# Paced operand work in a fused attention and two-layer gated network: rates by kind of pass, earlier stores, charged borders, and another order in the prologue

## The chip, the cores and the metric

One core of one Trainium2 chip runs the whole program. The metric is the device time in microseconds (us) of one execution; lower is better. A run gives one time, and the median of the runs is compared. A profiled execution has a time of its own and a span, which runs from the first to the last instruction that the profiler saw.

## The reference

Chunked attention over 4 batches, 8 heads, 768 positions and head size 64, then two networks over the 3072 tokens of width 512.

```python
for c in range(24):                       # chunks of 32 queries
    k_full = concat([mem_k, k[l_start:r_end]])   # 8 memory keys, 16 left, 32, 8 right
    a = softmax(scale * q_c @ k_full.T)
    out[c] = a @ v_full
x = out.transpose(0, 2, 1, 3).reshape(3072, 512)
x = (sigmoid(x @ w_gate) * (x @ w_val)) @ w_out        # d_ff 1536
h = x @ w_in                                           # d_ff 2048
y = (h * sigmoid(h)) @ w_out2
```

q, k and v are float32; the weights are float64, arrive as pairs of 32-bit words, and the kernel turns each into a float32.

## The kernel before

**Operands.** A product is made of three TensorE passes: each operand is split into a high part (rounded to the fp32r type by a cast on ScalarE) and a low part (the difference, on VectorE), and high x high, high x low and low x high are added in PSUM. `Unit.rebias` (a Prelu on ScalarE, L124) and `Unit.join` (a shift, L134, and a shift with or, L137, on VectorE) make a float32 of it; `high` and `rest` split it.

**Stages.** The first network takes the tokens in blocks of 512. Four of its six blocks go the plain way (the loop at L1260): for each of 12 column tiles f a gate projection (`proj`, PSUM tile pg), a value projection (pv), the sigmoid, the product `gated`, and the out projection of the tile before (`emit_out1`, PSUM tile y). The attention of the coming block is worked off beside it at fixed steps (`run_events`: "meet" is scores, maximum and difference, then "exp", "norm", and "turn", a transpose on TensorE). The last two blocks of the first network, and all of the second, go in `pair2` (products into c, L1060) and `out2` (products into o, L1224): seven products of sums of quarter matrices instead of eight, in the manner of Strassen. Passes are numbered by b (-1 for the first network's rest, 0 to 2 for the second network) and by p; for b = -1 each p has a pass of kind "g" and one of kind "v".

**Operand work.** The sums of weights that these products need (S1 to S4) are made on the way, in small portions between the other work, and stored to DRAM: in blocks 1 to 3 for the first network's weights (`PairC`) and w_in (`Pair2` "i"), in the passes b = -1 and b = 0 for w_out2 (`Pair2` "o", tiles stg_w2o, fo, coo, DRAM tensor w2o_d). A planner, `Pace`, hands out the portions while the program is written out, so it sets nothing but the order of instructions on each engine. A generator `steps` of an item yields the cost in us of its next VectorE portion, or None to end the step. `Pace.go(us)` is called once in each third of a tile, and at three beats of each pass. It first issues the stores that are LAG steps old, adds us to a credit (`due`, at most 3.2), and lets the item go on while the credit pays. The casts need a free one of four (in stage one five) tiles co: a tile is free again REST = 3 steps after its store was issued.

A "Pair2" item is charged 1.15 us for each of two joins, 0.8 for each of two halves of the sums, 0.7 for three low parts and 0.4 for the last. `early` issues the next item's Prelus, before its first join.

`Pace.finish` hands out what is left at once. For w_out2 it stands ahead of pass b = 0, p = 6 (L1337), since the memory of the prep pool is needed there:

```python
if b == 0 and p == NPAIR - 2:
    prep.finish()
    pp_cm.__exit__(None, None, None)
```

**A pass.** `pair2` emits, in order: product c1 with A11 and its copy s1 (ScalarE, L1095); c3 with S1 and its copy s5 (L1099), to which GpSimd adds s1 (L1100); c2 with S2 and the sum u2 (VectorE, L1025); beat 0; c1 goes on with A12; c2 with S3 and the sum into s5; beat 1; c3 with S4; c2 with A22; beat 2. A product is 6 matmuls. c1 goes on in the same PSUM tile that s1 is copied from, and c2 in that which u2 is read from. The weights of a pass come from DRAM through a ring of five buffers (wr, `next_granule`); loads, stores and ring loads all go through SyncE's queue (SP) in the order of the program. `tail_of` gives the next pass the work that forms an operand of `out2`; where there is none it gives a function that does nothing:

```python
return lambda: None
```

In `pair2` the result of that call is `rest`, and beat 0 hands out 0.0 where `rest` holds.

**Prologue.** The first four attention tiles and the first weights are done in an order written out by hand (PROLOGUE); after it x is split in `x_high` (ScalarE, L561) and `x_low` (VectorE, L564) and the first tile's two projections run together in `proj_both` (L346). units[1] is the value weight of tile 0. `Pace` is made at block 1; its first act is `ones[0].ahead()`, which on GpSimd adds up the high and low part of two gate weights (L670).

**Borders.** At f = 11 of a block `split_x` splits the next block's x (four casts on ScalarE, L96, and four differences on VectorE, L99); at f = 0 of the next block four y tiles are copied (L908, L910) and stored (L911).

Of the kernel before, what the change touches and what calls it, by code (L numbers as in the profile page):

```python
# [22 lines left out]
KT = DM // P  # L23
# [9 lines left out]
NPAIR = NF2 // 2  # L33
# [18 lines left out]
DVE_US = {"meet": 2.1, "norm": 1.75}  # L52
PREP1, PREP_END, PREP1X = 1.9, 130, 1.2
PREP2 = {"g": (0.7, 2.2, 1.5), "v": (0.8, 1.1, 0.3), "l": (0.8, 2.3, 1.7)}
# [3 lines left out]
def moe_kernel(ctx: ExitStack, tc: tile.TileContext, qh, kh, vh, wg, wv, wo, w2i, w2o, out):  # L58
# [282 lines left out]
    def proj_both(os, ws, x, n):  # L341

        steps = [(i, kt, p) for i in range(2) for kt in range(KT) for p in ((0, 0), (1, 0))]
        steps += [(i, kt, (0, 1)) for i in range(2) for kt in range(KT)]
        for i, kt, (pw, px) in steps:
            nc.tensor.matmul(  # L346
                os[i][:, :n],
                ws[i][:, pw, kt * P : (kt + 1) * P],
                x[kt][:, px, :n],
                start=kt == 0 and (pw, px) == (0, 0),  # L350
                stop=kt == KT - 1 and px == 1,
            )
# [34 lines left out]
    with tc.manual_schedule():  # L387
# [182 lines left out]
        x_low(0)  # L570
        units[1].high()
        x_high(2)
        units[1].rest()
        x_high(3)
        x_low(1)
# [69 lines left out]
        class PairC:  # L645
# [33 lines left out]
            def ahead(self):  # L679
                even, odd = (w_t[2 * self.p + j][:, "gv".index(self.k)] for j in range(2))  # L680
                self.store(A11, even)
                self.store(A22, odd[:, :, 256:])
                self.t = [
                    p1.tile([P, 512], F32, tag=f"u{j}", name=f"tc{self.k}{self.p}_{j}")
                    for j in range(2)
                ]
                self.whole(self.t[0], even, nc.gpsimd)
                self.whole(self.t[1], odd, nc.gpsimd)
# [30 lines left out]
        class Pair2:  # L719
# [31 lines left out]
            def steps(self, pace):  # L751
                k, p = self.k, self.p
                if not self.ready:
                    self.rebias()
                    yield None
# [39 lines left out]
        class Pace:  # L795

            LAG, REST = 2, 3

            def __init__(self, items, tags):
# [8 lines left out]
                if ones:  # L808
                    ones[0].ahead()

            def early(self):
                coming = self.urgent or self.items
                if coming and isinstance(coming[0], Pair2):
                    coming[0].rebias()
# [35 lines left out]
            def go(self, us):  # L850
                self.step += 1
                while self.fifo and self.fifo[0][0] <= self.step - self.LAG:
                    self.put()
                self.due = min(self.due + us, 3.2)
                while self.next is not False and self.next <= self.due:
# [186 lines left out]
        def pair2(b, p, fill, tail, kind=""):  # L1042
# [43 lines left out]
            def beat(n):  # L1086
                if b < 0 or b == 0 and p < NPAIR - 2:
                    us = PREP2[kind if kind else "l"][n]
                    prep.go(0.0 if rest and n == 0 or b < 0 and p == 0 and kind == "g" else us)
# [6 lines left out]
            if tail and early:  # L1096
                tail()()
# [29 lines left out]
            def tail_of():  # L1127
# [6 lines left out]
                return lambda: None  # L1134
# [125 lines left out]
        for bi, n in enumerate(BLOCKS1[:NB1]):  # L1260
            last = bi == NB1 - 1
            if bi == 1:
                prep = Pace(items, ["stg2", "stg3", "co0", "co1", "co2"])
            for f in range(NF1):
                it = 3 * (bi * NF1 + f)

                def steps(i):
# [3 lines left out]
                    else:  # L1271
                        prep.go((PREP1 if it + i < PREP_END else PREP1X) - sum(DVE_US.get(w, 0) for w, t in events.get(it + i, [])))
# [12 lines left out]
                else:  # L1285
                    proj(psg, U1["g", f].u, x, n, late=(0, 1) if f == 0 else (1, 0) if bi else None)
# [38 lines left out]
        prep = Pace([Pair2("o", p, pool) for p in range(NPAIR)], ["co0", "co1", "co2", "co3"])  # L1325
        xgen = iter(())
        for b in range(-1, NB2):
# [14 lines left out]
            tail()()  # L1342
# [3 lines left out]
            def beside(m):  # L1346
                nonlocal xgen
                if b + 1 == NB2:
                    return
                if m == 0:  # L1350
# [81 lines left out]
```

## Time and profile before

| | us |
|---|---|
| median of 3 runs | 1113.5 |
| lowest and highest run | 1112.88, 1116.63 |
| the profiled execution, time | 1114.81 |
| the profiled execution, span | 1113.0 |
| TensorE busy | 1087.2 |
| VectorE busy | 759.7 |
| ScalarE busy | 533.6 |
| GpSimd busy | 97.0 |

The profiled execution lies 1.31 us above the median of the runs, and 1.81 us of it lie outside the span. Engines are named PE (TensorE; PEld is its weight load), DVE (VectorE), ACT (ScalarE), POOL (GpSimd) and SP (SyncE); a q behind the name is the engine's issuing of a DMA or its wait ahead of an instruction. A wait in brackets names the idle time of the engine ahead of the row and what ended it.

### The profile page before, as it was taken

What the parts mean: (1) busy time and instruction counts of PE and PEld (TensorE: products, weight loads), DVE (VectorE), ACT (ScalarE), POOL (GpSimd) and SP (SyncE); (2) the same over time, 40 slices, a digit from 0 to 9 for tenths busy, and PEclk for the clock granted to TensorE, in tenths of its full rate; (3) what the DMA queues carried; (4) which work ended last, traced back from release to release, by engine and by line L of the source; (5) the groups of instructions that cost most, each with busy time, mean ns of one, the idle gap of its engine ahead of it and who ended that gap; (6) DMA issues with size and microseconds to landing.
All of it is one profiled execution on the core that took longest, in us unless ns stands there. A gap on an engine that the chain in (4) does not pass through costs nothing.

```text
span 1113.0 us, 18985 instructions
## 1 busy us (share of the span) xinstructions
PE 1087.2 (98%) x7580; PEld 890.2 (80%) x7580; DVE 759.7 (68%) x1132; ACT 533.6 (48%) x791; POOL 97.0 (9%) x74
## 2 busy tenths in 40 slices
PE   7999999999999999999999999699999999999998
PEld 4888888878888788888888888588888888888887
DVE  8988776777766766657769866468833489443665
ACT  6767555454445453443444556354443454344442
POOL 0000001002111001011111011000011110011000
PEclk9999999999999999999999999899999999999999
DMA  8788788697986897678998699765765766655551
GB/s 319 259 276 302 263 298 296 224 323 271 320 294 222 308 303 275 223 266 311 301 315 313 206 336 336 278 268 190 244 200 194 274 217 218 208 199 208 203 218 71
DMA packets 106248, 288.03 MB, mean 259 GB/s; under 512 B 8624, under 2 KB 39344, under 8 KB 95408
## 3 DMA queue, kind: packets, MB, share of 16 engines
q1 hardware_dynamic: 105872, 286.43, 73.5%
q8 instruction: 60, 0.98, 0.4%
q10 hardware_dynamic: 288, 0.39, 0.1%
q14 instruction: 28, 0.23, 0.1%
HBM read 210.24 MB, written 76.55 MB: 258 GB/s over the span
## 4 chain that ended last, share of the span: by engine, by line
PE 93%; DVE 3%; ACT 2%; DMA 1%; issue 0%; SPq 0%; DVEq 0%; ACTq 0%
PE o L1224 21%; PE c L1060 20%; PE pg L359 11%; PE pv L359 11%; PE y L104 4%; PE y L106 4%; PE y L108 4%; PE sx L308 1%; PE sx L220 1%; PE o_-1_0_6435 L1224 1%; PE o_-1_1_6436 L1224 1%; PE c_-1_4g L1060 1%; PE c_-1_2v L1060 1%; PE c_-1_5v L1060 1%; PE c_-1_5g L1060 1%; PE c_-1_3v L1060 1%
## 5 line engine op out<-in xcount | busy, mean ns | idle before, releaser
L1060 PE MATMUL c<-xp,wr 128*128 128x512 f32 x1008 | 231.3, 392 | 10.3 <-ACT s L1095 10.3
L1060 PEld LDWEIGHTS c<-xp,wr 128*128 128x128 f32 x1008 | 190.7, 189 | 50.3 <-ACT s L1095 10.7
L1224 PE MATMUL o<-gf,wr 128*128 128x512 f32 x1008 | 229.0, 389 | 0.0
L1224 PEld LDWEIGHTS o<-gf,wr 128*128 128x128 f32 x1008 | 189.3, 188 | 39.2
L359 PE MATMUL pv<-x,w 128*128 128x512 f32 x564 | 139.0, 396 | 1.1 <-DVE sg L374 1.1
L359 PE MATMUL pg<-x,w 128*128 128x512 f32 x564 | 136.2, 391 | 0.9 <-ACT sg L369 0.9
L1167 DVE TENSOR_TENSOR gf<-g,gf 128x1024 fp32r<-128x1024 f32 x84 | 104.0, 1241 | 46.6 <-ACT gf L1163 46.1
L1163 ACT CAST gf<-g 128x1024 fp32r<-128x1024 f32 x84 | 88.1, 1052 | 87.1 <-PE o L1224 69.8
L359 PEld LDWEIGHTS pg<-x,w 128*128 128x128 f32 x564 | 105.5, 188 | 23.4 <-ACT sg L369 1.4
L359 PEld LDWEIGHTS pv<-x,w 128*128 128x128 f32 x564 | 104.1, 188 | 24.8 <-DVE sg L374 2.1
L1025 DVE TENSOR_TENSOR s<-c,s 128x512 f32<-128x512 f32 x48 | 33.1, 690 | 53.0 <-PE c L1060 52.6
L1100 POOL TENSOR_TENSOR s<-s,s 128x512 f32<-128x512 f32 x24 | 34.3, 1430 | 333.2 <-ACT s L1099 333.2
L1028 DVE TENSOR_TENSOR g<-g,g 128x1024 f32<-128x1024 f32 x48 | 59.6, 1241 | 0.0
L369 ACT ACTIVATE sg<-pg 128x512 f32<-128x512 f32 x48 | 28.6, 596 | 59.9 <-PE pg L359 46.8
L379 DVE TENSOR_TENSOR g<-sg,g 128x512 fp32r<-128x512 f32 x48 | 33.9, 706 | 34.3 <-ACT g L376 34.3
L376 ACT CAST g<-sg 128x512 fp32r<-128x512 f32 x48 | 29.8, 620 | 55.1 <-DVE sg L374 55.1
L1031 ACT ACTIVATE g<-s 128x512 f32<-128x512 f32 x48 | 30.3, 632 | 47.1 <-DVE s L1025 47.1
L1025 DVE TENSOR_TENSOR u<-c,s 128x512 f32<-128x512 f32 x24 | 16.6, 690 | 50.1 <-PE c L1060 46.6
L269 ACT ACT_TABLE_LOAD x21 | 26.9, 1283 | 36.6 <-DVE e L261 34.8
L104 PE MATMUL y<-g,wor 128*128 128x512 f32 x144 | 40.1, 400 | 0.0
L106 PE MATMUL y<-g,wor 128*128 128x512 f32 x144 | 38.7, 390 | 0.0
L108 PE MATMUL y<-g,wor 128*128 128x512 f32 x144 | 38.6, 390 | 0.0
(602 smaller groups left out, 1579.1 us busy)
## 6 DMA issues: line engine op xcount, KB each, us to landing
wr<-w2o_d SPq DMA_DIRECT2D x42, 1024.0 KB, 4.8
wr<-w2i_d SPq DMA_DIRECT2D x24, 1024.0 KB, 5.3
wor<-wo_d SPq DMA_DIRECT2D x36, 512.0 KB, 6.2
wr<-w2i_d SPq DMA_DIRECT2D x24, 768.0 KB, 4.5
w2o_d<-coo SPq DMA_DIRECT2D x56, 256.0 KB, 7.0
w2i_d<-coi SPq DMA_DIRECT2D x24, 512.0 KB, 6.2
wr<-wc_d SPq DMA_DIRECT2D x12, 1024.0 KB, 6.5
v<-in_vh_dram SPq DMA_DIRECT2D x21, 512.0 KB, 5.4
```

Of the source, the lines that this page charges most:

```text
L104: nc.tensor.matmul(o, w_hi, x_hi, start=first, stop=False)
L106: nc.tensor.matmul(o, w_hi, x_lo, start=False, stop=False)
L108: nc.tensor.matmul(o, w_lo, x_hi, start=False, stop=last)
L359: nc.tensor.matmul(o[:, :n], w[:, pw, kt * P : (kt + 1) * P], x[kt][:, px, :n], start=i == 0, stop=i == len(steps) - 1,)
L379: nc.vector.tensor_tensor(out=g[:, 1, :n], in0=sg[:, :n], in1=g[:, 0, :n].bitcast(F32), op=ALU.subtract)
L1025: nc.vector.tensor_tensor(out=o, in0=a, in1=b_, op=ALU.add)
L1028: nc.vector.tensor_tensor(out=o, in0=a, in1=b_, op=ALU.subtract)
L1060: nc.tensor.matmul(o, w[:, pw, m, kt * P : (kt + 1) * P], X[i][:, px, kt], start=first and j == 0, stop=j == 5, skip_group_check=not first,)
L1100: nc.gpsimd.tensor_tensor(out=s5, in0=s5, in1=s1, op=ALU.add)
L1163: nc.scalar.copy(f[:, 0], src)
L1167: nc.vector.tensor_tensor(out=f[:, 1], in0=src, in1=f[:, 0].bitcast(F32), op=ALU.subtract)
L1224: nc.tensor.matmul(c[at[i], dp], w[:, pw, pl, dp * P : (dp + 1) * P], f[:, px, pl], start=i in (A11, S1, S2) and pp == 0 and j == 0, stop= ...
```

## The change

It edits the planner, its rates, the prologue and two orders of matmuls.

- Rates: stage one's step goes from 1.9 to 2.15 us; a step with `split_x` is charged 2.4 more, the second step of tile 0 of a block 1.4 more. The passes of b = -1 and b = 0 get rates "g", "v" and "rest"; b = 0 takes "rest" for p = 0 and for a pass that really has a `rest`, else "g". `tail_of` returns None where there is nothing to do.
- `Pace` for w_out2 gets lag 1 instead of 2 and a credit of at most 2.8 instead of 3.2; a call with 0.0 now only issues stores, and `out2` of b = -1 makes three such calls. Prelus aren't issued at beat 2.
- Prologue: `x_high(2)` and `x_high(3)` go ahead of the value weight's cast, `x_low(1)` ahead of its low part. The first `ahead` goes from GpSimd to VectorE.
- `proj_both` takes the value weight's high parts for all four kt ahead of its low ones; in block 0 the gate projection takes the weight's low part last.

```diff
-DVE_US = {"meet": 2.1, "norm": 1.75}
-PREP1, PREP_END, PREP1X = 1.9, 130, 1.2
-PREP2 = {"g": (0.7, 2.2, 1.5), "v": (0.8, 1.1, 0.3), "l": (0.8, 2.3, 1.7)}
+DVE_US = {"meet": 2.1, "norm": 1.75, "split": 2.4, "y": 1.4}
+PREP1, PREP_END, PREP1X = 2.15, 130, 1.2
+PREP2 = {"g": (0.9, 2.6, 1.8), "v": (1.0, 1.3, 0.7), "rest": (0.0, 0.9, 1.3)}
...
     def proj_both(os, ws, x, n):
-        steps = [(i, kt, p) for i in range(2) for kt in range(KT) for p in ((0, 0), (1, 0))]
+        steps = [(0, kt, p) for kt in range(KT) for p in ((0, 0), (1, 0))]
+        steps += [(1, kt, p) for p in ((0, 0), (1, 0)) for kt in range(KT)]
         steps += [(i, kt, (0, 1)) for i in range(2) for kt in range(KT)]
...
         x_low(0)
+        x_high(2)
+        x_high(3)
         units[1].high()
-        x_high(2)
+        x_low(1)
         units[1].rest()
-        x_high(3)
-        x_low(1)
         units[2].rebias()
...
-                self.whole(self.t[0], even, nc.gpsimd)
-                self.whole(self.t[1], odd, nc.gpsimd)
+                self.whole(self.t[0], even, eng)
+                self.whole(self.t[1], odd, eng)
...
                 if not self.ready:
+                    while not pace.act:
+                        yield None
                     self.rebias()
...
-            LAG, REST = 2, 3
-            def __init__(self, items, tags):
+            REST = 3
+            def __init__(self, items, tags, lag, cap):
+                self.lag, self.cap, self.act = lag, cap, True
...
                 if ones:
-                    ones[0].ahead()
+                    ones[0].ahead(nc.vector)
...
-                if coming and isinstance(coming[0], Pair2):
+                if self.act and coming and isinstance(coming[0], Pair2):
                     coming[0].rebias()
...
-            def go(self, us):
+            def go(self, us, act=True):
                 self.step += 1
-                while self.fifo and self.fifo[0][0] <= self.step - self.LAG:
+                self.act = act
+                while self.fifo and self.fifo[0][0] <= self.step - self.lag:
                     self.put()
-                self.due = min(self.due + us, 3.2)
-                while self.next is not False and self.next <= self.due:
+                self.due = min(self.due + us, self.cap)
+                while us and self.next is not False and self.next <= self.due:
...
-                    us = PREP2[kind if kind else "l"][n]
-                    prep.go(0.0 if rest and n == 0 or b < 0 and p == 0 and kind == "g" else us)
+                    us = PREP2["rest" if rest or b == 0 and p == 0 else kind or "g"][n]
+                    prep.go(0.0 if b < 0 and p == 0 and kind == "g" else us, n < 2)
...
-                return lambda: None
+                return None
...
-                prep = Pace(items, ["stg2", "stg3", "co0", "co1", "co2"])
+                prep = Pace(items, ["stg2", "stg3", "co0", "co1", "co2"], 2, 3.2)
...
+                        if (f, i) == (NF1 - 1, 2) and not last:
+                            names.append("split")
+                        if (f, i) == (0, 1):
+                            names.append("y")
+                        us = PREP1 if it + i < PREP_END else PREP1X
+                        prep.go(us - sum(DVE_US.get(w, 0) for w in names))
...
-                    proj(psg, U1["g", f].u, x, n, late=(0, 1) if f == 0 else (1, 0) if bi else None)
+                    proj(psg, U1["g", f].u, x, n, late=(0, 1) if f == 0 else (1, 0))
...
-        prep = Pace([Pair2("o", p, pool) for p in range(NPAIR)], ["co0", "co1", "co2", "co3"])
+        prep = Pace([Pair2("o", p, pool) for p in range(NPAIR)], ["co0", "co1", "co2", "co3"], 1, 2.8)
...
+                if b < 0 and m in (3, 8, 14):
+                    prep.go(0.0)
```

## Rows read from the trace of the kernel before

**Rows 1.** The page: busy time of each engine, its share of the span, instructions.

```profile
PE 1087.2 (98%) x7580; PEld 890.2 (80%) x7580; DVE 759.7 (68%) x1132; ACT 533.6 (48%) x791; POOL 97.0 (9%) x74
```

**Rows 2.** TensorE's waits: us in total, times, longest.

```profile
PE c L1060 <- ACT s L1095: 10.3, 1, 10.3
...
PE pt L292 <- DVE e L287: 0.7, 3, 0.3
...
PE c_-1_4v L1060 <- ACT s_-1_4v L1095: 0.4, 1, 0.4
```

**Rows 3.** Stretches: length, busy time (instructions) by engine, clock, DMA share, GB/s.

```profile
464.54:582.43 117.89, 117.44 (x518) 96.73 (x517) 76.40 (x126) 47.26 (x82) 15.52 (x12) 1.00 0.85 294
...
639.65:728.39 88.74, 78.45 (x338) 64.51 (x337) 52.77 (x87) 43.25 (x73) 10.35 (x8) 0.94 0.87 304
804.55:880.71 76.16, 76.16 (x338) 63.10 (x337) 28.96 (x38) 31.21 (x50) 11.99 (x8) 1.00 0.59 200
```

**Rows 4.** Timeline, 696 to 713 us: start, length, engine, line, operation, tiles.

```profile
697.23 15.18 SPq L746 DMA_DIRECT2D w2o_d<-coo  x14
...
706.81 0.62 ACT L777 CAST coo<-fo 128x512 fp32r<-128x512 f32 x1 [7.81 <-DMA w2o_d<-coo]
...
710.51 0.58 ACT L1095 COPY s<-c 128x512 f32<-128x512 f32 x1
...
711.14 2.08 PE L1060 MATMUL c<-xp,wr 128*128 128x512 f32 x4 [10.29 <-ACT s L1095]
```

**Rows 5.** Stretches in the prologue and after the long wait.

```profile
25.00:29.30 4.30, 2.96 (x7) 2.38 (x8) 4.11 (x8) 4.12 (x7) 0.00 (x0) 0.60 0.77 287
...
705.20:715.40 10.20, 4.26 (x10) 3.43 (x11) 5.23 (x6) 4.46 (x8) 1.28 (x1) 0.50 0.81 276
```

**Rows 6.** Timeline of the prologue's end.

```profile
23.22 1.25 PE L346 MATMUL pg<-x,w 128*128 128x512 f32 x4 [0.40 <-ACT x L561]
26.34 2.08 PE L346 MATMUL pg<-x,w 128*128 128x512 f32 x4 [1.87 <-ACT x L561]
...
32.37 0.84 PE L359 MATMUL pg<-x,w 128*128 128x512 f32 x3
...
23.46 1.66 DVE L137 SCALAR_TENSOR_TENSOR t_wv<-stg_wv 128x512 int32<-128x512 int32 x1
...
22.55 1.14 ACT L561 CAST x<-x 128x512 fp32r<-128x512 f32 x2 [0.61 <-DVE x L317]
...
23.18 1.39 POOL L670 TENSOR_TENSOR tcg<-w 128x512 f32<-128x512 f32 x1 [21.87 <-DVE w L147]
```

**Rows 7.** The tile stg_wv up to 60 us: ns least, median, most.

```profile
L137 DVE SCALAR_TENSOR_TENSOR t_wv<-stg_wv x5: 692/693/1656, 23.5 to 54.5; 128x512 int32<-128x512 int32 x5
```

**Rows 8.** Timeline at the border of blocks 0 and 1, VectorE.

```profile
137.82 0.43 DVE L134 TENSOR_SCALAR stg_w2i<-stg_w2i 128x512 int32<-128x512 int32 x1 [2.74 <-DMA stg_w2i<-in_w2i_dram]
```

**Rows 9.** Timeline at the border of blocks 2 and 3.

```profile
354.35 2.92 PE L359 MATMUL pg<-x,w 128*128 128x512 f32 x12
...
353.32 2.18 ACT L96 CAST x<-x 128x512 fp32r<-128x512 f32 x4
...
367.23 1.29 DVE L670 TENSOR_TENSOR tc<-wor 128x512 f32<-128x512 f32 x2
...
367.98 0.33 SPq L883 DMA_DIRECT2D wor<-wo_d  x1
...
374.58 3.03 PE L359 MATMUL pg<-x,w 128*128 128x512 f32 x12 [0.95 <-ACT sg L369]
378.67 3.03 PE L359 MATMUL pv<-x,w 128*128 128x512 f32 x12 [1.06 <-DVE sg L374]
```

**Rows 10.** The page: a group of sums (busy, mean ns), and the stores of coo.

```profile
L1025 DVE TENSOR_TENSOR s<-c,s 128x512 f32<-128x512 f32 x48 | 33.1, 690 | 53.0 <-PE c L1060 52.6
...
w2o_d<-coo SPq DMA_DIRECT2D x56, 256.0 KB, 7.0
```

**Rows 11.** The tile stg_w2o: its loads, from issue to landing.

```profile
DMA to landing us min/median/max: 3.7/6.7/7.6
```

More of the change, by code (lines that the diff above doesn't have):

```diff
@@ L677, in begin, with ahead @@
                 self.whole(self.t[1], odd, nc.vector)
-            def ahead(self):
+            def ahead(self, eng=None):
+                eng = eng or nc.gpsimd
                 even, odd = (w_t[2 * self.p + j][:, "gv".index(self.k)] for j in range(2))
@@ L1096, in pair2 @@
             if tail and early:
-                tail()()
+                (tail() or int)()
             prod(c3, S1, True)
@@ L1271, in steps @@
                     else:
-                        prep.go((PREP1 if it + i < PREP_END else PREP1X) - sum(DVE_US.get(w, 0) for w, t in events.get(it + i, [])))
+                        names = [w for w, t in events.get(it + i, [])]
+                        if (f, i) == (NF1 - 1, 2) and not last:
[4 more added lines that the diff above has]
+                        prep.go(us - sum(DVE_US.get(w, 0) for w in names))
                     if xgen is not None and (it + i) % 3 != 1:
@@ L1341, in moe_kernel @@
                     tail = pair2(b, p, None, tail)
-            tail()()
+            (tail() or int)()
             if b < 0:
```

## The prediction

> **What bounds the kernel now.** I read the page first: TensorE is busy for 1087.2 of 1113.0 us [rows 1], so what a change of order can win is at most its 26 us of idle time, and what it loses to a lower clock. Then TensorE's waits [rows 2]: one of 10.3 us holds over a third of that; of the small ones two matter below, 0.7 and 0.4. Then stretches cut at the borders of the stages [rows 3]: a stage of eight passes takes 76.16 us where nothing is in the way (804.55 to 880.71), and the stage of b = 0, with the same matmuls, 88.74 us. The difference of 12.58 us is the largest thing to win. The timeline there [rows 4] shows whose it is: ScalarE sat idle 7.81 us for a store of coo to land, then did the last casts (L777), then the copy s1 (L1095) that TensorE needed before it could go on at 711.14, after 10.29 us. SyncE issued 14 such stores in 15.18 us. This is `finish`: the last item of w_out2 was not done when pass p = 6 came, and its casts, which need tiles whose stores have only just been issued, stand in ScalarE's queue ahead of s1. The other 12.58 - 10.29 = 2.29 us are clock: from 705.2 to 715.4 it was 0.50, the level of 1.2 GHz, after 4.3 us without a matmul [rows 5].
>
> The prologue's end comes second [rows 6]: the 24 matmuls of `proj_both` run from 23.22 to the next projection at 32.37, though at the usual pace (76.16 us for 336, 0.227 each) they take 5.4. TensorE waited 1.87 us for a cast of x, and the clock was 0.60 on the mean over the next 4.3 us [rows 5].
>
> **The planner.** I step its credit through the beats by hand. An item of w_out2 costs 2 x 1.15 + 2 x 0.8 + 3 x 0.7 + 0.4 = 6.4, eight cost 51.2. Before, `lambda: None` is a true value, so beat 0 hands out nothing in any pass with a predecessor: b = -1 gives 5 x (2.2 + 1.5) + 6 x (1.1 + 0.3) = 26.9, b = 0 gives 4.8 + 5 x 4.0 = 24.8. That is 51.7 for 51.2, and steps lost to busy tiles use up more than the rest: the last item's casts are left for `finish`, as the rows show. After, b = -1 gives 3 x 5.3 (g at p = 1, 3, 5) + 2 x 2.2 (p = 2, 4, with a real rest) + 6 x 3.0 = 38.3, b = 0 gives 3 x 2.2 + 3 x 5.3 = 22.5: 60.8 in all. Stepped through with the four tiles, the last low part falls in beat 2 of p = 4 and the last store in beat 0 of p = 5; `finish` finds nothing. The stores and the loads of the moved items are cheap here, since they aren't new.
>
> **Part by part.**
>
> *The wait at finish:* -12.6 us, idle time and clock together. If a remnant stayed and the clock alone came back it would be 2.3; I see none, so 12.6.
>
> *Prologue:* while GpSimd adds up a gate weight (23.18, 1.39 us), VectorE's L137 on the value weight takes 1.66 us instead of 0.69 [rows 6, 7], and on ScalarE the cast of that weight, and behind it those of x(2) and x(3), wait for it. With `ahead` on VectorE and x(2), x(3) first, ScalarE's casts run on from 22.55 at about 0.55 each [rows 6] and end at 24.75; the value weight is joined at 23.46 + 0.69 = 24.15, cast by 25.4, its low part done by 26.05. TensorE takes the gate's eight matmuls until 25.25, the value's eight until 27.2, then the eight with low x, the last of which are done at 27.35: an end near 29.0 instead of 32.4. The next projection needs its weight's high part: join after `x_low(3)`, 28.5, cast 29.1, so it starts near 29.1. That is -3.3 with the clock at its upper level throughout. If the clock falls as before (a mean of 0.60 over 4.3 us [rows 5] is 3.4 us at half, from about 25.9 on), 1.7 of this is lost: bounds -1.6 and -3.7 (all that 9.15 us exceed 5.44 by). The hole of 1.87 us ahead of the fall shrinks to 0.2, so I take -3.3. (The Trainium skill, TensorE: Matmul & The Clock Gate, Part 1, has the clock follow how busy the engine has lately been. By that rule the fall can also come from the thinly filled time before 23 us, which the change leaves, and the sum would be 1.7 smaller; no row tells the two apart.) The two additions moved to VectorE, some 0.65 each, fall at the start of block 1, where it waits 2.74 us for the first load of w_in [rows 8]; without that cover they cost 1.3.
>
> *Border of blocks 2 and 3:* the y stores stand behind a load of w_out (L883, 367.98) that waits for VectorE's L670 (367.23), and VectorE is late by the joins and sums handed out at that border; the sigmoid needs a y tile's buffer and TensorE waits 0.95 and 1.06 [rows 9]. With the charges these portions go elsewhere: two joins and four sums, some 3.8 us, leave the way between, so both waits go, -2.0. Against it, stepping stage one, the credit saved up at step 1 of that tile now pays a join, both sums and two casts ahead of `split_x`. The casts need the sums, and end 1.2 us later than now; x's first cast (353.32 now, [rows 9]) is then ready near 355.1, and the projection that starts at 354.35 waits 0.8, and 0.4 more at the transpose: +1.2, against two of the three waits at a transpose now (0.7 together, [rows 2]), some 0.5. Net -1.3; bounds -2.5 (no late casts) and +0.7 (late casts and the y stores still blocked). At the border of 1 and 2 a cast leaves the same chain: -0.3, the third of those waits.
>
> *Prelus not at beat 2:* the wait of 0.4 us at p = 4 [rows 2] is the copy s1 behind two Prelus: -0.4.
>
> *Matmul orders:* the same matmuls; nothing, beyond the prologue.
>
> *More work in b = -1:* per pass VectorE has four sums of 0.69 [rows 10], in "v" four products as long, and 5.3 or 3.0 of portions: 8.1 and 8.5 of the 9.52 us that 42 matmuls take. ScalarE is fuller, but not full (47.26 of 117.89 us now, [rows 3]). DMA: 2.1 MB of loads and about 2.0 MB of stores move into the stretch 464.5 to 582.4, which now moves 34.7 MB (294 GB/s, share 0.85, [rows 3]): 38.8 MB, 329 GB/s, share 0.95. It fits, narrowly. New waits of 0 to 5 us can follow (rival 1 has the place); I take 0.5.
>
> **Sum:** 12.6 + 3.3 + 1.3 + 0.3 + 0.4 - 0.5 = 17.4. The profiled execution would take 1114.81 - 17.4 = 1097.4; it lies 1.31 above the median of the runs shown, 1113.5, and against that the forecast is 1096.1 us.
>
> **Rivals.**
>
> 1. *The Prelu waits for its load (the side that is slower).* In the "g" passes of p = 1, 3, 5 the next item's load is handed out at beat 0 and its Prelus at beat 1 of the same pass; before, a whole pass lay between. By SyncE's order the load can go out 0.45 us into the pass; it lands in 6.7 us, at most 7.6 [rows 11], and ScalarE comes to the Prelus near 9.0. Behind them stand two sigmoids and the next pass's s1, which TensorE needs 13.6 us in (9.52 and 18 matmuls); so nothing is lost until a load takes 10 us. The fuller DMA speaks for it, the measured 7.6 against. At 13 us it costs 3 x 3 = 9, and 1105 comes out; from about 16 us on it takes back all 17.4, and each wait over 4.3 us brings the clock down as [rows 5] show (2.3 more each): at 17 us 3 x 9.3 = 27.9, some 1124. The same holds for casts that wait for stores: they now follow them by three beats, 9.5 us, against 7.0 [rows 10].
>
> 2. *The change doesn't do what it says:* an item is still open at p = 6, because a tile is busy where I counted it free. Then part of the wait stays; half of it gives 1096.1 + 6.3 = 1102.4.
>
> 3. *The clock falls in the prologue all the same:* against it that the hole ahead of the fall is nearly closed, for it that the matmuls before 23.22 [rows 6] stay as few as they were: 1096.1 + 1.7 = 1097.8.
>
> 4. *VectorE late through GpSimd.* Each pass has an addition on GpSimd of s1 to s5; portions moved into b = -1 can meet it and be held as L137 was, by 0.97 us [rows 7]. A portion of beat 2 held so ends about 4.5 us into the next pass, and u2, due at 5.4, takes 0.69: late by no more than 0.3 us. In eleven passes that is up to 3.3: 1099.4. (The Trainium skill, SBUF — State Buffer, "Who interferes with whom", says that a VectorE instruction with two SBUF inputs and a GpSimd one that reads SBUF exclude each other for a whole instruction. By that rule every sum and low part can be held, not L137 alone, which is why this rival has a chance of its own.)
>
> **How the numbers follow.** As forecast, with the small terms within their bounds (1093.7 to 1098): 0.62. Rival 3: 0.12. Rival 4: 0.07. Rival 2: 0.05. Rival 1 in part (1098 to 1108): 0.09; in full, slower: 0.04; near no change, from the same place: 0.01. The range of 8 in 10 takes in the first three and the mild part of rival 1: 1093.5 to 1101. A measurement of this kernel tells about 0.3%, 3.3 us, from no change: faster 0.95, same 0.01, slower 0.04.
>
> **What would show it.** In the profile after: the stage of b = 0 takes about 76.2 us from its first to its last c matmul, and no cast L777 waits for a store ahead of s1; the clock stays at 1.00 there. L137 on the first value weight takes 0.69 us, the first projection at L359 starts near 29. No wait of a projection on the sigmoid at the border of blocks 2 and 3, but one near 0.8 us on a cast of x. The stretch of b = -1 has a DMA share near 0.95. The forecast is wrong if waits on s1 show up in the passes after "g" of p = 1, 3 or 5, if `finish` still finds casts to do, or if the attention tiles' loads, which share SyncE's queue, come late in stage one.

## The result, and the profile after

The changed kernel takes 1100.06 us (median of 5 runs, 1099.36 to 1100.85) beside 1113.5 for the kernel before: a ratio of 0.9872, 95% interval 0.9853 to 0.989. That is 13.4 us less; the forecast was 17.4 less, and 1100.06 lies inside its range near the upper end. The profiled execution took 1100.55 us with a span of 1098.8. Line numbers have moved: L346 is now L347, L359 is L360, L561 is L562, L633 is L634, L641 is L642, L670 is L671, L777 is L781, L1025 is L1031, L1060 is L1066, L1095 is L1101, L1100 is L1106, L1167 is L1173, L1224 is L1230.

The page, busy time by engine, answers to [rows 1]:

```profile
PE 1085.0 (99%) x7580; PEld 888.0 (81%) x7580; DVE 758.0 (69%) x1134; ACT 534.1 (49%) x791; POOL 95.0 (9%) x72
```

TensorE's waits (us in total, times, longest) answer to [rows 2]:

```profile
PE c_-1_3g L1066 <- DVE u_-1_3g L1031: 0.9, 1, 0.9
PE c_-1_5g L1066 <- DVE u_-1_5g L1031: 0.9, 1, 0.9
...
PE pg L360 <- ACT x L96: 0.4, 1, 0.4
...
PE c L1066 <- ACT s L1101: 0.4, 2, 0.2
```

The wait of 10.3 us is gone, and five small waits for other engines that were not there before have come (the last row holds two); a sixth new one, 0.5 us in the attention's products px (L308), has no releaser in the profile. The stretches of [rows 3], cut at the same matmuls (columns as there), say where the time went:

```profile
460.35:579.75 119.40, 117.55 (x517) 96.69 (x517) 85.32 (x144) 49.42 (x87) 16.58 (x12) 1.00 0.91 315
636.98:714.14 77.16, 76.76 (x337) 62.91 (x337) 44.96 (x69) 39.04 (x65) 10.36 (x8) 1.00 0.87 297
790.30:866.46 76.16, 76.16 (x337) 63.06 (x337) 28.96 (x38) 31.24 (x50) 11.99 (x8) 1.00 0.59 199
```

Block 0's eight passes lost 11.58 us (88.74 to 77.16) and their clock is 1.00. The passes of b = -1 grew by 1.51 (117.89 to 119.40): VectorE has 18 instructions and 8.92 us more to do there. The start of that stretch moved from 464.54 to 460.35, 4.19 earlier, which is the prologue and stage one. So -4.19 + 1.51 - 11.58 = -14.26, and that is the whole difference of the two profiled executions, 1114.81 - 1100.55.

The prologue's end, the timeline of TensorE, VectorE and ScalarE, answers to [rows 6]:

```profile
24.67 2.30 PE L347 MATMUL pg<-x,w 128*128 128x512 f32 x8 [0.40 <-ACT x L562]
26.81 2.04 PE L347 MATMUL pv<-x,w 128*128 128x512 f32 x8
...
30.50 3.00 PE L360 MATMUL pg<-x,w 128*128 128x512 f32 x12
...
24.92 0.69 DVE L137 SCALAR_TENSOR_TENSOR t_wv<-stg_wv 128x512 int32<-128x512 int32 x1
...
24.00 2.19 ACT L562 CAST x<-x 128x512 fp32r<-128x512 f32 x4 [1.28 <-DVE x L317]
```

From the first matmul to the next projection it is 5.83 us in place of 9.15, without a hole; but the first matmul comes at 24.67, not at 23.22, and so the projection starts only 1.87 earlier. On the tile stg_wv L137 now takes 0.69 throughout, against the 1.66 of [rows 7]. The two additions that moved to VectorE cost nothing: at the start of block 1 it still waits 1.63 us for the load of w_in ([rows 8] have 2.74).

The border of blocks 2 and 3 (TensorE, ScalarE), against [rows 9]:

```profile
353.27 3.22 PE L360 MATMUL pg<-x,w 128*128 128x512 f32 x12 [0.41 <-ACT x L96]
...
372.75 2.88 PE L360 MATMUL pg<-x,w 128*128 128x512 f32 x12
375.47 2.89 PE L360 MATMUL pv<-x,w 128*128 128x512 f32 x12
...
351.56 1.14 ACT L781 CAST coi<-fi 128x512 fp32r<-128x512 f32 x2 [0.29 <-DVE fi L634]
352.60 2.18 ACT L96 CAST x<-x 128x512 fp32r<-128x512 f32 x4
```

The waits of 0.95 and 1.06 us are gone; the casts of coi stand ahead of x's casts, and the projection waits 0.41 us for them, as the forecast had it, at half its size.

Last, VectorE, GpSimd and TensorE where the new wait of 0.93 us arises (timeline, pass p = 3 "g"):

```profile
523.45 0.69 DVE L1090 TENSOR_TENSOR g-1_1_21_5887<-s_-1_2v,g-1_1_21_5887 128x512 f32<-128x512 f32 x1
524.05 1.84 DVE L634 TENSOR_TENSOR fo<-fo 128x256 f32<-128x256 f32 x2
525.82 0.68 DVE L1031 TENSOR_TENSOR u_-1_3g<-c_-1_3g,s_-1_3g 128x512 f32<-128x512 f32 x1
...
523.66 1.61 POOL L1106 TENSOR_TENSOR s_-1_3g<-s_-1_3g 128x512 f32<-128x512 f32 x1 [8.28 <-ACT s_-1_3g L1105]
...
526.55 1.66 PE L1066 MATMUL c_-1_3g<-xp-1_3_5399,wr 128*128 128x512 f32 x6 [0.93 <-DVE u_-1_3g L1031]
```

Two sums of w_out2 (L634), handed out at beat 2 of the v pass, stand ahead of u2. The first started 0.39 us after GpSimd began to add s1 to s5 and took 1.51 us; both took 1.84.

### The profile page after: what moved, and what is told of

Read it like the earlier page. It is cut to its first block, busy times and chain, and to the rows that moved or that the text cites. A ratio compares the mean times of both kernels' runs of the same rounds, so it can differ in the third digit from the quotient of the medians.

```text
span 1098.8 us, 18989 instructions
## 1 busy us (share of the span) xinstructions
PE 1085.0 (99%) x7580; PEld 888.0 (81%) x7580; DVE 758.0 (69%) x1134; ACT 534.1 (49%) x791; POOL 95.0 (9%) x72
## 4 chain that ended last, share of the span: by engine, by line
PE 94%; DVE 3%; ACT 1%; DMA 1%; issue 1%; DVEq 0%; ACTq 0%
PE o L1230 21%; PE c L1066 21%; PE pg L360 11%; PE pv L360 11%; PE y L104 4%; PE y L106 4%; PE y L108 4%; PE sx L308 1%; PE sx L220 1%; PE o_-1_1_6485 L1230 1%; PE o_-1_0_6484 L1230 1%; PE pt L292 1%; PE c_-1_5v L1066 1%; PE c_-1_4g L1066 1%; PE c_-1_3v L1066 1%; PE c_-1_2g L1066 1%
## 5 line engine op out<-in xcount | busy, mean ns | idle before, releaser
L1066 PE MATMUL c<-xp,wr 128*128 128x512 f32 x1008 | 229.6, 389 | 0.4 <-ACT s L1101 0.4
L1230 PE MATMUL o<-gf,wr 128*128 128x512 f32 x1008 | 229.0, 389 | 0.0
L1066 PEld LDWEIGHTS c<-xp,wr 128*128 128x128 f32 x1008 | 189.0, 188 | 40.4 <-ACT s L1101 1.2
L1230 PEld LDWEIGHTS o<-gf,wr 128*128 128x128 f32 x1008 | 189.2, 188 | 39.3
L360 PE MATMUL pv<-x,w 128*128 128x512 f32 x564 | 138.6, 394 | 0.0
L360 PE MATMUL pg<-x,w 128*128 128x512 f32 x564 | 136.4, 391 | 0.4 <-ACT x L96 0.4
L1173 DVE TENSOR_TENSOR gf<-g,gf 128x1024 fp32r<-128x1024 f32 x84 | 103.9, 1240 | 46.3 <-ACT gf L1169 45.9
L360 PEld LDWEIGHTS pg<-x,w 128*128 128x128 f32 x564 | 105.2, 188 | 23.4 <-ACT x L96 1.5
L360 PEld LDWEIGHTS pv<-x,w 128*128 128x128 f32 x564 | 104.1, 188 | 23.2 <-DVE sg L375 0.5
L1031 DVE TENSOR_TENSOR s<-c,s 128x512 f32<-128x512 f32 x48 | 33.2, 691 | 56.7 <-PE c L1066 52.6
L1106 POOL TENSOR_TENSOR s<-s,s 128x512 f32<-128x512 f32 x24 | 34.3, 1431 | 321.7 <-ACT s L1105 321.7
L1031 DVE TENSOR_TENSOR u<-c,s 128x512 f32<-128x512 f32 x24 | 16.6, 690 | 51.8 <-PE c L1066 44.7
L269 ACT ACT_TABLE_LOAD x21 | 26.9, 1283 | 31.5 <-DVE e L261 29.7
L671 POOL TENSOR_TENSOR tcv<-w 128x512 f32<-128x512 f32 x12 | 16.7, 1415 | 284.2 <-DVE fcg L634 284.2
L104 PE MATMUL y<-g,wor 128*128 128x512 f32 x144 | 40.0, 400 | 0.0
L375 DVE TENSOR_TENSOR sg<-pv,sg 128x512 f32<-128x512 f32 x48 | 32.9, 685 | 8.5 <-PE pv L360 6.4
```

Of the source, the lines that this page charges most:

```text
L104: nc.tensor.matmul(o, w_hi, x_hi, start=first, stop=False)
L360: nc.tensor.matmul(o[:, :n], w[:, pw, kt * P : (kt + 1) * P], x[kt][:, px, :n], start=i == 0, stop=i == len(steps) - 1,)
L1031: nc.vector.tensor_tensor(out=o, in0=a, in1=b_, op=ALU.add)
L1066: nc.tensor.matmul(o, w[:, pw, m, kt * P : (kt + 1) * P], X[i][:, px, kt], start=first and j == 0, stop=j == 5, skip_group_check=not first,)
L1106: nc.gpsimd.tensor_tensor(out=s5, in0=s5, in1=s1, op=ALU.add)
L1173: nc.vector.tensor_tensor(out=f[:, 1], in0=src, in1=f[:, 0].bitcast(F32), op=ALU.subtract)
```

## The experiments

Each median is compared with that of the kernel before on the same chip; two kernels ran once, and are read by their profiles.

**Three parts, one at a time.** The kernel before with one part of the change each: all that concerns w_out2's planner; the prologue with its matmul orders and the first `ahead`; stage one's rate and charges.

```diff
 e1_second_planner
-PREP2 = {"g": (0.7, 2.2, 1.5), "v": (0.8, 1.1, 0.3), "l": (0.8, 2.3, 1.7)}
+PREP2 = {"g": (0.9, 2.6, 1.8), "v": (1.0, 1.3, 0.7), "rest": (0.0, 0.9, 1.3)}
 ...
-                return lambda: None
+                return None
 ...
 e2_prologue
         x_low(0)
+        x_high(2)
+        x_high(3)
         units[1].high()
 ...
-                ones[0].ahead()
+                ones[0].ahead(nc.vector)
 ...
 e3_stage_one
-DVE_US = {"meet": 2.1, "norm": 1.75}
-PREP1, PREP_END, PREP1X = 1.9, 130, 1.2
+DVE_US = {"meet": 2.1, "norm": 1.75, "split": 2.4, "y": 1.4}
+PREP1, PREP_END, PREP1X = 2.15, 130, 1.2
 ...
```

> Kernel before with only the planner's part for w_out2: its rates, lag 1 and credit 2.8, no Prelu at beat 2, None from tail_of, three store-only calls in out2. Theory 'the wait at finish is the gain': the 12.6 us lost at p = 6 go, less about 2.5 for the new waits on u2 in passes p = 3 and 5 and for the casts ahead of s1 in b = 0; about 1103.5 us (-10), with no wait over 1 us on s1. Rival 'the parts help one another' (the prologue or stage one has to hand over earlier for the passes to be done in time): less than -7, and casts left at p = 6.

> Kernel before with only the prologue's part: x_high(2), x_high(3) and x_low(1) earlier, the matmul order of proj_both and of block 0, and the first addition of gate weights on VectorE. Theory 'the prologue is worth what I summed, and the changed kernel's profile merely began 1.4 us late': from the first to the 24th matmul of proj_both 6.0 us instead of 9.2, median -3.0 us, and the first matmul of proj_both anywhere between 23.2 and 24.7 in the span, as the first loads land. Rival 'the part itself delays the attention ahead of it': the first matmul at 24.6 again, median -1.7.

> Kernel before with only stage one's part: 2.15 us a step, split_x charged 2.4, the y copies 1.4. Theory: both waits of a projection at the border of blocks 2 and 3 go, a new one of about 0.4 on a cast of x and one near 190 us of 0.5 come: -1.5 to -2.0 us. Rival 'the waits there come from the loads, not from VectorE's portions': no change, and the waits of 0.95 and 1.06 stay.

The kernel before took 1113.67 us there. The planner alone gave 1104.9 (ratio 0.9923, 0.9907 to 0.9938), the prologue 1111.12 (0.9977, 0.9968 to 0.9986), stage one 1112.25 (0.9989, 0.9979 to 0.9999). Their sum is -8.8 - 2.55 - 1.4 = -12.75, beside -13.4 for the whole: the parts add up, and the planner carries two thirds. Each gave a little less than was expected of it. Two rows matter beyond that. The old `finish` was left in e2 and e3, and there TensorE's wait at it was 8.5 us each time, not 10.3. Here it is in e2, on the timeline:

```profile
637.47 61.36 PE L1062 MATMUL c<-xp,wr 128*128 128x512 f32 x270
707.34 17.69 PE L1062 MATMUL c<-xp,wr 128*128 128x512 f32 x66 [8.51 <-ACT s L1097]
724.87 10.36 PE L1226 MATMUL o<-gf,wr 128*128 128x512 f32 x45
```

The block's passes took 724.87 - 637.47 = 87.40 us there, so the stall cost 11.2 against the 12.6 of [rows 3]. And e1, with the old prologue, came late to its first projection without any change to it, and ended where the others do:

```profile
24.68 1.25 PE L346 MATMUL pg<-x,w 128*128 128x512 f32 x4
27.81 1.25 PE L346 MATMUL pg<-x,w 128*128 128x512 f32 x4 [1.88 <-ACT x L561]
28.89 2.00 PE L346 MATMUL pv<-x,w 128*128 128x512 f32 x8
...
32.54 2.88 PE L359 MATMUL pg<-x,w 128*128 128x512 f32 x12
```

What made it late lies ahead of these rows: the clock was 0.50 there, while TensorE did the attention's transposes and small products, and 1.00 again before the first matmul of the projection. In e4, a run further down that has the change's prologue, the same happened. The stretches (columns as in [rows 3]; the first row is e1, the other two are e4):

```profile
20.42:23.84 3.42, 3.42 (x133) 2.73 (x133) 2.63 (x5) 1.66 (x3) 0.00 (x0) 0.50 0.93 348
...
17.00:20.00 3.00, 1.49 (x69) 1.12 (x68) 2.83 (x8) 2.27 (x4) 0.00 (x0) 1.00 0.51 138
20.07:23.48 3.41, 3.33 (x133) 2.86 (x134) 2.50 (x5) 1.66 (x3) 0.00 (x0) 0.50 0.97 293
```

**What made the passes of b = -1 longer.** The changed kernel without GpSimd's addition in the passes of b = -1; this leaves out part of the computation: s1 isn't added to the product that becomes quarter 22 of g and v.

```diff
-            nc.gpsimd.tensor_tensor(out=s5, in0=s5, in1=s1, op=ALU.add)
+            if not kind:
+                nc.gpsimd.tensor_tensor(out=s5, in0=s5, in1=s1, op=ALU.add)
```

> Kernel after, with the addition of s1 to s5 on GpSimd left out in the passes of b = -1 (so the 22 quarter of their results lacks s1). Theory 'the addition on GpSimd holds VectorE's sums': the longest L634 falls from 1.51 to 0.43 us, the two waits of 0.9 on u2 at p = 3 and 5 go, and the stretch of b = -1 takes 117.6 us instead of 119.4; -1.5 us against after. Rival 'VectorE has too much to do there, GpSimd or no': the waits stay at 0.7 or more and the time is that of after, 1100.1.

1098.52 us, ratio 0.9864 (0.9848 to 0.988): 1.5 less than the changed kernel. Both waits on u2 are gone. The two sums at the same place (timeline), and the stretch of the passes (columns as in [rows 3]):

```profile
524.28 0.75 DVE L634 TENSOR_TENSOR fo<-fo 128x256 f32<-128x256 f32 x2
...
460.42:577.68 117.26, 117.26 (x517) 96.75 (x516) 82.82 (x144) 49.42 (x88) 0.00 (x0) 1.00 0.92 319
```

0.75 us in place of 1.84, begun 4.02 us into the pass as against 4.03, with the same work around it. So it is the overlap with GpSimd that holds VectorE, not too much work on VectorE: the passes take 2.14 us less and TensorE is busy in all of them.

The next run keeps all the work and moves it. In the changed kernel, beat 2 of a v pass hands out nothing, its share goes to beat 0 of the next pass, and in block 0 the casts wait for beat 0 or 1.

```diff
-PREP2 = {"g": (0.9, 2.6, 1.8), "v": (1.0, 1.3, 0.7), "rest": (0.0, 0.9, 1.3)}
+PREP2 = {"g": (1.6, 2.6, 1.8), "v": (1.0, 1.3, 0.0), "rest": (0.1, 0.9, 1.3)}
 ...
-                        while pace.busy():
+                        while pace.busy() or not pace.cast:
 ...
+                    prep.cast = b < 0 or n < 2
```

> The changed kernel with three places of the second stage's plan altered: the third beat of a v pass hands out nothing (its 0.7 goes to the first beat of the next pass), and in block 0 ScalarE's casts of w_out2 wait for the first or second beat. Theory, that what the change lost again in the passes is two portions put where the next pass needs the engine at once (a join of sums on VectorE beside GpSimd's addition, 0.93 us in each of two passes; casts on ScalarE ahead of s1, about 1.0 us in block 0): both go, the passes of block -1 take 117.6 us and those of block 0 76.2 to 76.4, the time is 1097.0 to 1097.6. Rival, that VectorE and ScalarE have too much to do in these passes wherever it is handed out: the waits of TensorE come back at another product with the same sum, the time is 1099.5 to 1100.5.

1097.21 us, ratio 0.9848 (0.9835 to 0.9861), as the theory had it. Its stretches of b = -1 and of block 0:

```profile
460.39:577.36 116.97, 116.97 (x517) 96.83 (x516) 84.21 (x144) 49.90 (x89) 16.58 (x12) 1.00 0.91 318
634.58:710.80 76.22, 76.22 (x337) 62.91 (x336) 43.22 (x69) 39.76 (x67) 10.37 (x8) 1.00 0.87 299
```

TensorE is busy in the whole of both. The 2.4 and 0.9 us by which they are shorter than in the changed kernel came from where the portions stood, not from how many there were.

**Which line removed the wait.** First the stores: the changed kernel with lag 2 and a credit of 3.2 for w_out2, as before.

```diff
-        prep = Pace([...], ["co0", "co1", "co2", "co3"], 1, 2.8)
+        prep = Pace([...], ["co0", "co1", "co2", "co3"], 2, 3.2)
```

> The changed kernel with the stores of w_out2's pairs two beats behind and the cap at 3.2, as before. Stepped by hand, the last store is then handed out at p = 5's second beat, still ahead of the last item's finish. Theory, that the wait went because all eight items end before p = 6, not because stores leave a beat sooner: 1099.5 to 1100.6, the same. Rival, that the sooner stores removed the wait: part of its 8 to 10 us comes back, 1104 or more.

1101.36 us, ratio 0.9885 (0.9872 to 0.9897), not told apart from the changed kernel's 0.9872; 0.8 above what was expected. No wait at `finish`: block 0 takes 76.16 us. Against that stands a wait of 1.28 us in `out2` of b = -1, where an operand comes late from VectorE. The sooner stores did not remove the wait.

Then the truth value alone, in the kernel before:

```diff
-                    tail()()
+                    (tail() or int)()
 ...
-                return lambda: None
+                return None
 ...
```

> The kernel before with one thing changed: a pass that leaves nothing for the next one returns None in place of an empty function, so that the first beat after it is not set to zero. The old rates then hand out about 9.3 us more in all, and stepped by hand the last item ends at p = 5's second beat. Theory, that the wait was this lost credit alone: the wait is gone and with it 8 to 10 us, 1103.5 to 1105.5 beside 1113.5, as much as the whole new second plan gave (1104.9). Rival, that the new rates and their placement are needed: more portions at the first and last beats of the passes bring new waits of 0.5 us and more in most odd passes, and the time is 1107 to 1111.

1109.1 us, ratio 0.9953 (0.9938 to 0.9968): 5.0 us, half of what the theory gave. The time is the rival's, but the reason is another. The wait at `finish` is gone. TensorE's waits and, on the timeline, SyncE, ScalarE and TensorE in block 0 show two others:

```profile
PE c L1060 <- ACT s L1095: 5.6, 2, 4.0
```

```profile
648.25 0.94 SPq L119 DMA_DIRECT2D stg_w2o<-in_w2o_dram  x2
...
656.12 0.67 ACT L124 ACTIVATE stg_w2o<-stg_w2o 128x512 f32<-128x512 f32 x1 [3.38 <-DMA stg_w2o<-in_w2o_dram]
657.40 0.65 ACT L124 ACTIVATE stg_w2o<-stg_w2o 128x512 f32<-128x512 f32 x1 [0.61 <-DMA stg_w2o<-in_w2o_dram]
657.95 0.57 ACT L1095 COPY s<-c 128x512 f32<-128x512 f32 x1
...
658.57 20.73 PE L1060 MATMUL c<-xp,wr 128*128 128x512 f32 x84 [3.98 <-ACT s L1095]
680.96 43.98 PE L1060 MATMUL c<-xp,wr 128*128 128x512 f32 x192 [1.66 <-ACT s L1095]
```

This is rival 1 of the prediction, in the other kernel. The load of the next item is handed out at beat 1 and its Prelus at beat 2; they reach ScalarE ahead of the next pass's s1 and sit there until the load lands, some 8 us after its issue (648.25 to 656.12). The whole pass stands behind them. The two waits are 5.6 us, and block 0 took 83.94 us (640.84 to 724.78), 7.8 above the floor of 76.16: in the first wait the clock fell, and it was 0.50 from 658.16 to 661.58. So the truth value and one more line were put into the kernel before: no Prelu at beat 2.

```diff
                 if not self.ready:
+                    while not pace.act:
+                        yield None
                     self.rebias()
 ...
-                if coming and isinstance(coming[0], Pair2):
+                if self.act and coming and isinstance(coming[0], Pair2):
 ...
```

> The kernel before with two things changed: a pass that leaves nothing returns None, and the first Prelu of a w_out2 item is handed out at a first or second beat alone; rates, lag, cap and everything else as before. Theory, that the run with None alone lost 5.6 us of its gain again because the Prelus of the last two items came one beat after their loads were issued (8 us before landing): held to the next pass's first beat they find their data, the waits of 4.0 and 1.7 us go, and the time is 1102.8 to 1104.4 beside 1113.5 to 1114.1, so that the new rates carry nothing of the gain. Rival, that the old rates put some other portion ahead of a product as soon as the Prelu is out of the way: waits of TensorE of 2 us and more remain in block 0, 1106 to 1109.

1102.68 us, ratio 0.9897 (0.9881 to 0.9914), 0.1 below the theory's band: 10.9 us with the old rates, by medians more than the 8.8 of the whole new planner (e1), though the two intervals overlap a little. The profiles say the same: the passes of b = -1 and block 0 take 118.35 and 76.16 us here, 119.41 and 77.16 in e1. Block 0, from the timeline, and the one wait that is left in the passes of b = -1 (0.4 in [rows 2]):

```profile
558.13 1.66 PE L1064 MATMUL c_-1_4v<-xp-1_4_5417,wr 128*128 128x512 f32 x6 [1.00 <-ACT s_-1_4v L1099]
...
639.87 76.32 PE L1064 MATMUL c<-xp,wr 128*128 128x512 f32 x336
716.03 76.32 PE L1228 MATMUL o<-gf,wr 128*128 128x512 f32 x336
```

716.03 - 639.87 = 76.16: the floor. Last, that kernel with the change's prologue and stage-one charges, which is the whole change but for its second-stage rates, lag, cap, extra store turns and the rule that a call with 0.0 only issues stores. Its diff against e9 is that of e2 and e3.

> The run with None and the held Prelu, with the change's prologue and stage-one charges added: the whole change but for the new rates of the second stage, their lag and cap, the first beats without hand-outs, and the three extra turns in the output. Theory, that the new rates cost 1.5 to 2.5 us (the sums beside GpSimd's addition and the casts ahead of s1) and give nothing that the other two don't: 1113.6 - 10.9 - 2.55 - 1.4 = 1098.8, between 1098.0 and 1099.6, with one wait of about 1.0 us left in the passes of block -1. Rival, that the rates are needed once the prologue and stage one are changed as well: 1100.0 or more.

1098.25 us, ratio 0.9856 (0.9833 to 0.988). The forecast by addition was 1098.8. The new rates and what came with them show no gain, and cost 1.8 us as far as medians of different chips tell; the intervals of this ratio and of the change's overlap. In the profiles the passes of b = -1 take 118.39 us here and 119.40 in the changed kernel, block 0 76.16 and 77.16: 2.0 us less. Which of the pieces left out costs it, no run tells.

**The prologue, piece by piece.** The changed kernel with one piece undone in each: the old order of x's copies; the first `ahead` on GpSimd; the old order of `proj_both`.

```diff
 e8_old_x_order
-        x_high(2)
-        x_high(3)
         units[1].high()
-        x_low(1)
+        x_high(2)
         units[1].rest()
+        x_high(3)
+        x_low(1)
 ...
 e10_gpsimd_ahead
-                    ones[0].ahead(nc.vector)
+                    ones[0].ahead()
 ...
 e11_old_matmul_order
-        steps = [(0, kt, p) for kt in range(KT) for p in ((0, 0), (1, 0))]
-        steps += [(1, kt, p) for p in ((0, 0), (1, 0)) for kt in range(KT)]
+        steps = [(i, kt, p) for i in range(2) for kt in range(KT) for p in ((0, 0), (1, 0))]
```

> The changed kernel with the prologue's copies of x in the old order, between the parts of the value weight; the order of the matmuls and the engine of the first ahead stay as changed. Theory, that the order of the copies carries the prologue's gain: TensorE waits for x copies 2 and 3 at the value projection's second half again (1.9 us in the profile of before), the time is 1101.5 to 1102.5. Rival, that the new order of matmuls alone carries it, since it takes the value weight later: 1099.8 to 1100.5.

> The changed kernel with the first preparation of a border operand back on GpSimd. Theory, that VectorE's 1.66 us in place of 0.69 for the value weight's L137 came from GpSimd running beside it: it is 1.5 to 1.7 us again, the value weight's cast ends some 0.5 us later, and the next projection starts 6.1 to 6.4 us after the first projection's first matmul, not 5.83. Rival, that the slow instruction came from something else in the old order: 0.69 stays, and 5.8 us.

> The changed kernel with the old order of the first projection's matmuls (for each slice of x the weight's high part, then its low part). Theory, that the order of matmuls gives little by itself: the value weight's low part is ready 0.6 us after its high part, so TensorE waits once for 0.3 to 0.5 us, and the next projection starts 6.1 to 6.4 us after the first matmul, not 5.83. Rival, that the order gives nothing: 5.8 to 5.9 us; or that it carries the gain: 7 us and more.

e8 took 1101.41 us (ratio 0.9885, 0.9871 to 0.99), by its interval not told apart from the changed kernel; e10 took 1102.41 and e11 1100.09 in one execution each. So the profiles have to tell. In e8 the wait for x came back at half its size:

```profile
24.44 1.26 PE L347 MATMUL pg<-x,w 128*128 128x512 f32 x4 [0.40 <-ACT x L562]
26.60 1.26 PE L347 MATMUL pg<-x,w 128*128 128x512 f32 x4 [0.90 <-ACT x L562]
...
31.37 2.88 PE L360 MATMUL pg<-x,w 128*128 128x512 f32 x12
```

From the first matmul to the projection that is 6.93 us, 1.10 more than the 5.83 of the change. In e10, VectorE, GpSimd and TensorE:

```profile
24.81 1.67 DVE L137 SCALAR_TENSOR_TENSOR t_wv<-stg_wv 128x512 int32<-128x512 int32 x1
...
24.52 1.41 POOL L671 TENSOR_TENSOR tcg<-w 128x512 f32<-128x512 f32 x1 [23.21 <-DVE w L147]
...
24.57 2.29 PE L347 MATMUL pg<-x,w 128*128 128x512 f32 x8 [0.40 <-ACT x L562]
27.18 2.36 PE L347 MATMUL pv<-x,w 128*128 128x512 f32 x8 [0.32 <-ACT w L144]
...
31.33 3.02 PE L360 MATMUL pg<-x,w 128*128 128x512 f32 x12
```

L137 is slow again, and nothing but the engine of that addition was changed: 6.76 us from 24.57 to 31.33, 0.93 more, and above the 6.1 to 6.4 that were expected. In e11:

```profile
23.79 2.30 PE L346 MATMUL pg<-x,w 128*128 128x512 f32 x8 [0.40 <-ACT x L561]
...
30.13 2.88 PE L359 MATMUL pg<-x,w 128*128 128x512 f32 x12
```

6.34 us, 0.51 more. So, by one profile each, the order of the copies and the engine of `ahead` carry the prologue's gain about equally, and the order of matmuls a smaller share.

## Why the prediction was right, and where its sizes were off

The mechanism was right in each of the three parts, and the sum was 3.1 us too large by the profiled executions (17.4 against 14.26). The remaining 0.8 of the 4.0 us between 1096.1 and 1100.06 is that the profiled execution of before lay 1.31 above its median, and that of after 0.49. The terms:

- **Finish, -12.6 forecast, -11.58 measured.** Nothing was left to hand out (rival 2 did not happen), no cast waits for a store, and the clock is 1.00, all as forecast. The step "I see none, so 12.6" was mis-sized by 1.0: casts handed out at beat 2 of p = 1 and 3, right behind the sums that they need, stand ahead of s1 (0.17 and 0.23 us of waits), and with them block 0 takes 77.16 and not 76.16 us; moved away (e5) it takes 76.22. The term was also read from one execution with a long stall: two others paid 11.2 (e2) and as much (e3, 87.36 us).
- **Prologue, -3.3 forecast, -1.87 in the profiles, -2.55 by e2's medians.** What the copies do was right: 5.83 us from the first matmul, and the forecast had 5.9 (23.22 to 29.1). The mis-sized step is that it took 23.22 as given. In five profiles with the old prologue the first matmul started between 23.22 and 24.68, and the projection between the 32.37 of [rows 6] and 33.10 (e7): the four that started by 23.82 lost clock behind the hole, and the fifth (e1) had lost it before, so that its hole came at the upper level. In six with the change's prologue the first matmul started between 24.23 and 24.88, the projection follows it by 5.83 or 5.84 us, and a late start is paid in full: it starts between 30.06 and 30.72. The medians of these two groups, 32.65 and 30.51, are 2.14 apart.
- **Border of blocks 2 and 3, -1.3 forecast, -2.1 measured.** The same two matmuls lie at 344.52 and 385.14 before, at 342.88 and 381.41 after: 40.62 against 38.53 us. Both waits went, and the late cast cost 0.41 where 0.8 was reckoned. The rest of stage one gave 0.2 (4.19 - 1.87 - 2.09), against 0.3.
- **More work in b = -1, +0.5, with -0.4 for the Prelu, +0.1 in all; +1.51 measured.** This is the one place where a rival came true, rival 4, at its place and for its reason, in two passes instead of eleven. "Late by no more than 0.3 us" failed: it was 0.93. The argument let the held portion end 4.5 us into the pass; it ended 5.87 in (524.05 + 1.84 against a pass that starts at 520.02). VectorE was behind by the two joins of beat 1 before it got there: without the hold, in e4, the portion still ends 4.77 in. The hold itself, 1.09 us, was near the 0.97 forecast. The DMA share came out at 0.91, where 0.95 was forecast.
- **Rival 1** did not happen in the changed kernel, though the loads of stg_w2o now land after 3.6, 7.7 and 9.5 us (least, median, most; 3.7, 6.7, 7.6 in [rows 11]), close to the 10 us that it named as its threshold. In e7 its mechanism came true in block 0, and cost 7.8 us, 5.6 of it waits. The forecast gave the loss of clock to waits over 4.3 us; in e7 a wait of 3.98 brought it too.
- **Rival 3** did not happen in the changed kernel's profile, nor behind the first matmul in any of nine profiles with the change's prologue, whole or with one piece undone. In e11 the first matmul came at 23.79, as early as in the runs of the old order that lost clock, and its clock was 1.00 all through the projection (24.4 to 31.5). But the thin time alone can bring the clock down, as e1 and e4 show: in e4 TensorE was busy for 1.49 of the 3.00 us from 17 on, and the clock was 0.50 from 20.07 to 23.48. The transposes there start at 20.15 in e4 and at 20.16 in e11, and the first matmul 0.90 later than in e11. The longer reach that the Trainium skill's rule allowed (TensorE: Matmul & The Clock Gate, Part 1), a fall from the thin time alone, shows in these two traces. e11 was as thinly busy (1.50 of 3.00) and kept the upper level; no run shows what decides it.

What the prediction missed altogether is that the new rates weren't needed. It stepped the planner's credit by hand and found that a function that does nothing counts as true; but it did not give the lost credit, some 9 us, back to the old rates. With them the old rates leave nothing for `finish` (e7), and with the rule on the Prelus as well they give 10.9 us (e9).

## What to carry to other kernels

A planner that writes out an order loses time silently where a credit is dropped, so count what it hands out against what there is before rates are tuned; here one truth value and one rule on where a waiting instruction may stand gave 10.9 us with the old rates, and no run shows a gain of the new ones. Place a portion by what the next product needs from that engine first, not by how much the engine has to do in the stage: an instruction that waits for a load, or one on VectorE that meets GpSimd's work, belongs behind the copies and sums that TensorE waits for. Don't read a gain at the start of a program from one profile, neither from time zero nor from the first matmul on: the first matmul moves by more than a microsecond, and from it to the projection the same old prologue took 9.15 us before and 7.86 in e1. Take the start of the projection in several profiles.

The version with the portions moved (e5, 1097.21 us beside 1114.08) was by its ratio the fastest of those that do all the work; the change without its new rates (e12, 1098.25 beside 1114.85) comes next, and their intervals overlap. Both together weren't tried.

## What was not expected of the hardware

Two VectorE instructions that met a GpSimd addition took about a microsecond more each: the sum L634 1510 ns against 406 at least in the same kernel, and 427 at most in e4, where GpSimd adds nothing in b = -1; L137 1.67 us against 0.69 (e10). GpSimd's own addition was lengthened less, to 1.61 us where it takes 1.29 to 1.30 in nine of the twelve passes of b = -1. The Trainium skill has the two exclude each other for a whole instruction (SBUF — State Buffer, "Who interferes with whom"); both runs agree with that: the held instruction ended 0.3 and 0.55 us after GpSimd's. Why the first matmul starts at 23.2 us in one execution and at 24.9 in another is known in part. In e1 and e4 the low clock ahead of it made it late. In the profile after and in e2, e5, e6 and e10 TensorE stood idle for 0.50 to 1.05 us in the middle of the products px (L308), with no releaser that the profile shows; before, e3, e7, e9 and e11, which start by 23.82, have neither. All five with that idle time have the change's order of copies and matmuls, but so has e12, which is without it (24.23); no run tells whether the change has a part in it.
